# Attention and a two-layer MLP: the third tile by seven block products, with its loads, scores and totals in another order

## The chip, the core and the metric

The kernel runs on one core of a Trainium2 chip. The metric is the device time of one execution in microseconds (us). The core has five engines that run beside each other, each through its own queue in program order: TensorE (PE, matrix products into the accumulation memory PSUM), VectorE (DVE), ScalarE (ACT), GpSimd (POOL) and SyncE (SP), which in this kernel issues nearly all transfers between the device memory and the core. An instruction that waits holds up everything behind it in its queue.

## The reference

`q`, `k` and `v` have 8 batches, 8 heads, 576 rows and 64 columns. Each head attends within chunks of 64 rows, 9 chunks to a batch. The result, 4608 rows of 512, goes through two weight matrices with an exact GELU between them.

```python
scores = scale * np.matmul(q_c, k_c.transpose(0, 1, 2, 4, 3))   # chunks of 64 rows
scores = scores - np.max(scores, axis=-1, keepdims=True)
attn = np.exp(scores)
attn = attn / (np.sum(attn, axis=-1, keepdims=True) + 1e-09)
out = np.matmul(attn, v_c)
# x: (4608, 512), the heads side by side
h = x @ w_in                                                   # 512 -> 2048
g = 0.5 * h * (1.0 + erf(h * inv_sqrt2))
return (g @ w_out).astype(np.float32)                          # 2048 -> 512
```

## The kernel before

**Tiles.** The 4608 rows are worked in 9 tiles of 512 rows. Tile `t` from 0 to 7 holds the first 8 chunks of batch `t`; tile 8 holds the ninth chunk of all batches. The code runs a loop over `t` from 1 to 8, with tile 0 ahead of it. In each pass the PE does two long products for tile `t`:

- mm1 (`mm1_slot`, L414): 16 groups of 4 matmuls, each group 128 of the 2048 columns of `h`; ACT takes a group's PSUM bank through the Gelu into `h` (L421). The banks come from `ps_mm`, which has three.
- mm2: `h` times `w_out`. Tiles 0 to 2 do it directly (`mm2_slot`, L550): 16 slots of 4 matmuls of 512 columns; four slots make one block of 128 rows, which `rows_out` copies out of PSUM (ACT for the first three blocks, DVE for the fourth, L572) and `store` (L567) writes. Tiles 3 to 8 do it with `mm2_seven` (L476): a Winograd-style scheme with seven block products instead of eight, each of 16 matmuls of 256 columns (L519). It needs sums of blocks of `h`, made by DVE during mm1 (`g_sum`, L455), and sums of blocks of `w_out`, made once during mm1 of tile 1 (`weight_sum`, L444).

**Attention for later tiles.** The attention of tile `n = t + 1` is worked in between the matmuls of tile `t`. Its steps are: load `q` and `k` (`load_qk`, L103), cast to bf16 on POOL (`pool_cast_qk`), transpose by a DMA (`flip`, L191, one each for q and k), scores (`quad_S`, 64 small matmuls, L227), `exp` on ACT (L234), partial sums on DVE (L249, L252), totals and their reciprocals (`quad_total`, DVE L265 and L267 with small ACT copies L262 and L272 between them), spreading (`quad_rc`, L276), V (`load_v_rows`, cast by POOL, L200), attention times V (`quad_av`, L283) and the scaled result into `x` (`quad_x`, DVE L290), which mm1 of tile `n` reads.

**What sets the order.** Each engine's queue is in the order in which the code writes the instructions. Within mm1 and mm2 that order is written by hand: the dictionary `e1` says which steps stand ahead of which group of mm1, `e2` which stand ahead of which step of mm2. `phase` (L596) walks through both. At the head of each pass stand the transfers, all on SP's queue. Only the buffers are given out by the framework: a tile of a pool gets one of the pool's buffers when its former content has been read for the last time. The output buffers `y` (`ypool`) are four.

At the head of pass 1 the code puts on SP's queue: transpose of q of tile 2, half of V of 2, transpose of k of 2, three stores of tile 0 (`held`), the other half of V, then q and k of tile 3, q and k of tile 4, the transposes of tile 3, V of tile 3. The fourth row block of tile 0 is done inside mm1 of tile 1 (`last_av`), and its store stands behind all of these. Pass 2 begins with the transposes of tile 4.

In passes 1 and 2 the attention of tiles 2 and 3 is done wholly within mm2 of the tile before, and the scores of tile 4 stand in the last quarter of mm2 of tile 2 (`e2[12]`), its totals at group 3 of mm1 of tile 3 (`e1[3]`). From pass 3 on the scores of tile `t + 2` stand at the start of mm2 of tile `t`, its totals at step 10 of it, and the AV of tile `t + 1` at its start.

**The end.** The 512 rows of tile 8 go to eight separate places of 64 rows, four to a block. `store_block` writes four pieces for each of the first three blocks on SP; `last_piece` writes the last block, in two parts, half on SP and half on ACT's queue.

Of the kernel before, what the change touches and what calls it, by code (L numbers as in the profile page):

```python
# [11 lines left out]
def kernel(  # L12
# [9 lines left out]
    nc = tc.nc  # L22
    P = 128
    f32 = mybir.dt.float32
# [397 lines left out]

    NQ = 4
    T0 = 2
    joint = {T0: 3 * NQ}

    HF = FF // 2
    HD = d_model // 2
# [47 lines left out]
    def mm2_seven(t, hooks):  # L476

        st = tiles[t]

        def raw(r, c):  # L480
            return lambda f, m: st["h"][:, HF * c + f, HD * r + P * m:HD * r + P * (m + 1)]

        def summed(i):
            n = HF // 2
            return lambda f, m: st["S", i][f // n][:, f % n, P * m:P * (m + 1)]

        bank, kept = {}, {}

        def keep(name, of):
            kept[name] = ypool.tile([P, HM, HD], f32, tag="y", name="kept")  # L490
            nc.scalar.copy(kept[name][:], bank[of][:])  # L491

        def done(r, c, of, plus):
            y_sb = ypool.tile([P, HM, HD], f32, tag="y", name="y_sb")
            nc.vector.tensor_tensor(y_sb[:], bank[of][:], kept[plus][:], op=ADD)  # L495
            store_block(t, r, c, y_sb)

        def last():
            y_sb = ypool.tile([P, HM, HD], f32, tag="y", name="y_sb")
            nc.scalar.copy(y_sb[:], bank["a"][:])  # L500
            store_block(t, 1, 0, y_sb)

        steps = [("a", raw(0, 0), w_block(0, 0), lambda: keep("p1", "a")),
                 ("b", raw(0, 1), w_block(1, 0), lambda: done(0, 0, "b", "p1")),
                 ("a", summed(2), t_sum(2), lambda: keep("u2", "a")),
                 ("d", summed(1), t_sum(1), lambda: keep("p5", "d")),
                 ("a", summed(3), t_sum(3), lambda: done(1, 1, "a", "p5")),
                 ("d", summed(4), w_block(1, 1), lambda: done(0, 1, "d", "u2")),
                 ("a", raw(1, 1), t_sum(4), last)]
        for s, (name, left, right, then) in enumerate(steps):  # L510
            fresh = name not in bank
            for m in range(HM):
                for u in hooks.get(HM * s + m, ()):
                    u()
                if fresh and m == 0:
                    pool, tag = (ps_mm, "mm") if name == "d" or t == NT - 1 else (ps_tp, "tp")
                    bank[name] = pool.tile([P, HM, HD], f32, tag=tag, name="y_ps")
                for f in range(HF):
                    nc.tensor.matmul(bank[name][:, m], left(f, m), right[:, f],  # L519
                                     start=(fresh and m == 0 and f == 0),  # L520
                                     stop=(f == HF - 1), skip_group_check=True)
                if t == NT - 1 and s == len(steps) - 1:
                    last_piece(t, m, bank["a"][:, m])
            if not (t == NT - 1 and s == len(steps) - 1):
# [12 lines left out]

    def last_piece(t, m, y_ps):
        y_sb = ypool.tile([P, HD], f32, tag="y", name="y_sb")
        n = HD // 2  # L540
        if m == 0:
            nc.scalar.copy(y_sb[:], y_ps)
        else:
            nc.vector.tensor_copy(y_sb[:, 0:n], y_ps[:, 0:n])
            nc.scalar.copy(y_sb[:, n:HD], y_ps[:, n:HD])
        for i in range(P // CH):
            m0 = ((HM + m) * (P // CH) + i) * S + MT
            (nc.sync if i == 0 else nc.scalar).dma_start(out[m0:m0 + CH, 0:HD], y_sb[i * CH:(i + 1) * CH])

    def mm2_slot(t, ms, qt):  # L550
        st = tiles[t]
        if qt == 0:
            pool, tag = (ps_tp, "tp") if joint.get(t) == ms * NQ else (ps_mm, "mm")
            st["y_ps", ms] = pool.tile([P, d_model], f32, tag=tag, name="y_ps")
        y_ps = st["y_ps", ms]
        for f in range(qt * FF // NQ, (qt + 1) * FF // NQ):
            nc.tensor.matmul(y_ps[:], st["h"][:, f, ms * P:(ms + 1) * P], w_out_sb[:, f, :],  # L557
                             start=(f == 0), stop=(f == FF - 1))
        if qt == NQ - 1:
            if t > 0 or ms < 3:  # L560
                rows_out(t, ms)
# [93 lines left out]
    with tc.manual_schedule():  # L655
# [184 lines left out]
_INS = ['q', 'k', 'v', 'moe_w_in', 'moe_w_out']  # L840
_OUTS = [((4608, 512), 'float32')]
# [25 lines left out]
```

## Time and profile before

| | |
|---|---|
| median of 3 runs | 285.04 us (282.73 to 286.26) |
| the profiled execution's own time | 286.06 us |
| its span in the profile | 284.0 us |
| PE busy | 270.3 us, 95% |
| ACT, DVE, POOL busy | 180.7, 159.3, 91.7 us |
| read and written | 36.70 MB and 9.44 MB |

All times of the trace are from one execution and count from the start of its span. The granted clock of PE is given as a share of full speed. A line such as `L421` is a line of the kernel. In lists of waits, the engine and line behind an arrow are what ended an idle time.

### The profile page before, as it was taken

How to read it: one execution, taken by the hardware profiler on the slowest of the kernel's cores; microseconds unless marked ns; L12 is line 12 of the kernel's file. 1: busy time of each engine (PE TensorE's matmuls, PEld its weight loads, DVE VectorE, ACT ScalarE, POOL GpSimd, SP SyncE). 2: the span in 40 equal slices, each digit the busy share in tenths (PEclk: the TensorE clock that was granted, in tenths of full speed). 3: DMA queues.
4: the chain of work that ended last, by engine and by line, in shares of the span. 5: the costliest groups of instructions: out<-in, count | busy, mean ns of one | idle time of the engine just before them, and what ended most of it. 6: DMA issues, size and time to landing. Idle time of an engine off the chain costs nothing.

```text
span 284.0 us, 6437 instructions
## 1 busy us (share of the span) xinstructions
PE 270.3 (95%) x2589; PEld 160.7 (57%) x2589; DVE 159.3 (56%) x267; ACT 180.7 (64%) x370; POOL 91.7 (32%) x146
## 2 busy tenths in 40 slices
PE   6799999999999999799999999999999999999991
PEld 2464455444444444248844874587458745864781
DVE  5865358835900299448915992598159816311620
ACT  3766758877647667666676657757775766347410
POOL 6868778831542206304404610451011000000000
PEclk9999999999999999899999999999999999999998
DMA  7999998999789799999999998979430310130024
GB/s 222 253 360 402 393 362 234 226 254 239 179 235 244 238 262 240 241 212 255 220 285 237 168 204 177 176 168 260 107 84 2 113 35 2 39 111 0 2 46 102
DMA packets 122477, 53.89 MB, mean 190 GB/s; under 512 B 97872, under 2 KB 118352, under 8 KB 122448
## 3 DMA queue, kind: packets, MB, share of 16 engines
q1 hardware_dynamic: 122288, 53.36, 72.8%
q8 instruction: 20, 0.33, 0.5%
q10 hardware_dynamic: 160, 0.13, 0.2%
q14 instruction: 9, 0.07, 0.1%
HBM read 36.70 MB, written 9.44 MB: 162 GB/s over the span
## 4 chain that ended last, share of the span: by engine, by line
PE 87%; ACT 3%; DVE 2%; DMA 2%; POOL 2%; SPq 1%; issue 1%; DVEq 0%; ACTq 0%
PE h_ps L419 41%; PE y_ps L519 25%; PE y_ps L557 11%; PE y_ps L593 3%; PE h_ps L409 2%; DMA arrival<-in_k_dram 2%; POOL v_bd L169 2%; PE s_ps L227 1%; PE av_ps L283 1%; SPq L114 1%; PE tp L175 1%; ACT h L421 1%; DVE x L290 1%; PE av_ps L374 1%; ACT y_sb L572 1%
## 5 line engine op out<-in xcount | busy, mean ns | idle before, releaser
L419 PE MATMUL h_ps<-x,w_in_sb 128*128 128x512 bf16 x548 | 121.9, 383 | 2.2 <-ACT h L421 2.2
L421 ACT ACTIVATE h<-h_ps 128x512 bf16<-128x512 f32 x137 | 80.9, 598 | 38.0 <-PE h_ps L419 37.7
L419 PEld LDWEIGHTS <-w_in_sb 128*128 128x128 bf16 x548 | 54.0, 99 | 67.7 <-issue 5.0
L164 POOL CAST q_nat<-arrival 128x512 bf16<-128x512 f32 x31 | 19.9, 682 | 62.9 <-DMA arrival<-in_q_dram 41.9
L557 PE MATMUL y_ps<-w_out_sb,h 128*128 128x512 bf16 x144 | 32.4, 379 | 0.0
L519 PEld LDWEIGHTS <-h 128*128 128x128 bf16 x288 | 27.9, 98 | 5.1 <-issue 1.2
L200 POOL CAST v_nat<-arrival 128x1024 bf16<-128x1024 f32 x14 | 15.0, 1075 | 48.4 <-DMA arrival<-in_v_dram 30.2
L461 DVE TENSOR_TENSOR s_sb<-h 128x2048 bf16<-128x2048 bf16 x6 | 7.4, 1226 | 35.8 <-ACT h L421 35.8
L491 ACT COPY kept<-y_ps 128x512 f32<-128x512 f32 x18 | 10.6, 586 | 23.2 <-PE y_ps L519 22.0
L653 ACT ACT_TABLE_LOAD x18 | 23.1, 1283 | 1.1 <-PEq L851 0.7
L519 PE MATMUL y_ps<-w_out_sb,h 128*128 128x256 bf16 x192 | 22.0, 272 | 0.7 <-DVE x L290 0.5
L557 PEld LDWEIGHTS <-h 128*128 128x128 bf16 x144 | 13.5, 98 | 15.5 <-issue 0.2
L519 PE MATMUL y_ps<-v_bd,k_bd 128*128 128x256 bf16 x192 | 21.9, 273 | 0.0
L162 POOL CAST k_nat<-arrival 128x512 bf16<-128x512 f32 x28 | 21.1, 785 | 0.9 <-DMA arrival<-in_k_dram 0.9
L290 DVE TENSOR_TENSOR x<-av_ps,rc 128x512 bf16<-128x512 f32 x28 | 18.5, 682 | 4.8 <-PE av_ps L283 4.5
L519 PEld LDWEIGHTS <-k_bd 128*128 128x128 bf16 x192 | 18.8, 98 | 2.2
L252 DVE TENSOR_REDUCE part<-pt 128x16 f32<-128x512 bf16 x28 | 19.2, 686 | 1.0
L495 DVE TENSOR_TENSOR y_sb<-y_ps,kept 128x512 f32<-128x512 f32 x18 | 12.2, 678 | 12.9 <-PE y_ps L519 7.3
L474 DVE TENSOR_TENSOR k_bd<-h 128x1024 bf16<-128x1024 bf16 x12 | 9.2, 770 | 15.1 <-ACT h L421 15.1
L262 ACT COPY part<-part 32x32 f32<-32x32 f32 x56 | 12.3, 219 | 6.8 <-DVE part L252 6.0
L249 DVE STREAM_TRANSPOSE pt<-pT 128x256 f32<-128x256 f32 x28 | 12.2, 435 | 7.5 <-ACT pT L234 7.5
L234 ACT ACTIVATE pT<-s_ps 128x512 bf16<-128x512 f32 x28 | 14.8, 600 | 0.0
(97 smaller groups left out, 302.8 us busy)
## 6 DMA issues: line engine op xcount, KB each, us to landing
out_dram<-y_sb SPq DMA_DIRECT2D x32, 256.0 KB, 2.8
arrival<-in_v_dram SPq DMA_DIRECT2D x58, 128.0 KB, 3.3
arrival<-in_k_dram SPq DMA_DIRECT2D x28, 256.0 KB, 6.4
arrival<-in_q_dram SPq DMA_DIRECT2D x7, 1024.0 KB, 7.6
arrival<-in_moe_w_out_dram SPq DMA_DIRECT2D x4, 1024.0 KB, 11.7
arrival<-in_moe_w_in_dram SPq DMA_DIRECT2D x6, 512.0 KB, 7.8
arrival<-in_v_dram SPq DMA_DIRECT2D x28, 64.0 KB, 2.7
arrival<-in_q_dram SPq DMA_DIRECT2D x4, 256.0 KB, 5.0
```

The costliest lines, as they stand in the source:

```text
L162: copy(st[nm][:, :, g], st[nm + "f"][:, :, g].rearrange("p (q r) d -> p q r d", r=2))
L164: copy(st[nm][:, g].rearrange("p j r d -> p r j d"), st[nm + "f"][:, 2 * g:2 * g + 2])
L200: copy(st["v"][:, r::2], st["vf"][:, r::2])
L234: nc.scalar.activation(pT[:].rearrange("p u (c j) -> p u c j", j=J), s_ps[g2][c][:].rearrange("p u (j c) -> p u c j", j=J), Act.Exp, scale ...
L252: nc.vector.tensor_reduce(st["part", g2][:, c, :, :, 0], pt[:].rearrange("p n e u -> p n u e"), axis=mybir.AxisListType.X, op=mybir.AluOpT ...
L262: nc.scalar.copy(part[g2][QD * s:QD * (s + 1), :, :, :, 1], part[g2][QD * o:QD * (o + 1), :, :, :, 0])
L290: nc.vector.tensor_tensor(x.rearrange("p n (e u) -> p n e u", u=2), st["av"][g2][c][:].rearrange("p n (e u) -> p n e u", u=2), st["rc", 2 ...
L419: nc.tensor.matmul(h_ps[:], w_in_sb[:, ks, f * P:(f + 1) * P], tiles[t]["x"][:, ks, :], start=(ks == 0), stop=(ks == KS - 1))
L421: nc.scalar.activation(tiles[t]["h"][:, f, :], h_ps[:], Act.Gelu)
L519: nc.tensor.matmul(bank[name][:, m], left(f, m), right[:, f], start=(fresh and m == 0 and f == 0), stop=(f == HF - 1), skip_group_check=True)
L557: nc.tensor.matmul(y_ps[:], st["h"][:, f, ms * P:(ms + 1) * P], w_out_sb[:, f, :], start=(f == 0), stop=(f == FF - 1))
L653: nc.scalar.activation(act_scratch[:], rest[:, 0:1], func)
```

## The change

It alters the order of work around tiles 1 to 3, and how the last tile is stored.

- **Tile 2 by seven products.** `phase` is called with `seven=t >= T0`, so that mm2 of tile 2 goes through `mm2_seven` too. The special bank of `joint` goes.
- **Head of pass 1.** SP's order is now: q and k of tile 3, the transposes of tile 2, all of V of tile 2, the three stores of tile 0, the transposes of tile 3, q and k of tile 4, V of tile 3. POOL casts q and k of tile 3 ahead of V of tile 2.
- **Scores.** The scores of tile 3 stand at step 13 of mm2 of tile 1 (they stood at step 0 of mm2 of tile 2), and the table load for the Gelu moves behind them, to step 15. Pass 2 has the steps of the later passes: AV of tile 3 and scores of tile 4 at the start of mm2, the totals of tile 4 at step 10.
- **Totals.** The totals of tile 3 stand at group 6 of mm1 of tile 2, its spreading at group 8. In all passes from there on the first sum of `h` stands at group 10 of mm1 in place of 9.
- **Banks.** In `mm2_seven` the banks of tile 7 come from `ps_mm`. In tile 8 the bank `a` becomes a pair of banks from `ps_at`, and copies and sums of it go by halves.
- **The last stores.** Blocks of tile 8 go out in two transfers instead of four, one on SP, one on ACT's queue. The last block is copied in halves of 128 columns by DVE and ACT, stored by SP and ACT.

```diff
+        apart = t == NT - 1
+
+        def fresh_bank(name):
+            if apart and name == "a":
+                pair = [ps_at.tile([P, HD], f32, tag="at", name="y_ps") for _ in range(HM)]
+                bank[name] = [(slice(m, m + 1), pair[m][:].unsqueeze(1)) for m in range(HM)]
+                return
+            pool, tag = (ps_tp, "tp") if name != "d" and t + 2 < NT else (ps_mm, "mm")
+            bank[name] = [(slice(0, HM), pool.tile([P, HM, HD], f32, tag=tag, name="y_ps")[:])]
...
         def done(r, c, of, plus):
             y_sb = ypool.tile([P, HM, HD], f32, tag="y", name="y_sb")
-            nc.vector.tensor_tensor(y_sb[:], bank[of][:], kept[plus][:], op=ADD)
+            for m, y_ps in bank[of]:
+                nc.vector.tensor_tensor(y_sb[:, m], y_ps, kept[plus][:, m], op=ADD)
             store_block(t, r, c, y_sb)
...
-        for m in range(HM):
+        for i, eng in enumerate((nc.sync, nc.scalar)):
+            b0 = HM * r * (P // CH) + i
+            eng.dma_start(out_b[b0:b0 + 3:2, MT:S, cols].rearrange("b p d -> p b d"), y_sb[i * CH:(i + 1) * CH])
+
+    out_b = out.rearrange("(b s) d -> b s d", s=S)
+
+    def last_piece(t, m, y_ps):
+        n = HD // HM
+        b0 = (HM + m) * (P // CH)
+        for c, (copy, eng) in enumerate(((DV, nc.sync), (AC, nc.scalar))):
+            y_sb = ypool.tile([P, n], f32, tag="y", name="y_sb")
+            copy(y_sb[:], y_ps[:, n * c:n * (c + 1)])
             for i in range(P // CH):
-                m0 = ((HM * r + m) * (P // CH) + i) * S + MT
-                nc.sync.dma_start(out[m0:m0 + CH, cols], y_sb[i * CH:(i + 1) * CH, m])
...
+                eng.dma_start(out_b[b0 + i, MT:S, n * c:n * (c + 1)], y_sb[i * CH:(i + 1) * CH])
...
             if t == 1:
-                flip(2, "q")
-                load_v_rows(2, (0,))
-                flip(2, "k")
+                for nm in "qk":
+                    load_qk(3, nm)
+                flip_qk(2)
+                load_v_rows(2)
                 for ms, y_sb in held:
                     store(0, ms, y_sb)
                 held.clear()
-                load_v_rows(2, (1,))
+                pool_cast_qk(3)
+                flip_qk(3)
             elif t == T0:
                 flip_qk(t + 2)
             if n < NT:
                 cast_v_rows(n, PO)
-            if t == 1:
-                bring_qk(t + 2)
-                bring_qk(t + 3)
-                flip_qk(t + 2)
-            if t > 1 and t + 3 < NT:
+            if t + 3 < NT:
                 bring_qk(t + 3)
...
-                e2 = {0: [exp, lambda: quad_S(n)], 3: [total], 5: [gelu],
+                e2 = {0: [exp, lambda: quad_S(n)], 3: [total],
                       7: [av, lambda: quad_x(n, 0, 0)]
                          + [u for m in range(1, G)
-                            for u in (lambda m=m: quad_rc(n, m // 2, m % 2), lambda m=m: quad_x(n, m // 2, m % 2))]}
-            elif t == T0:
-                e2 = {0: [exp, lambda: quad_S(n)], 3: [total],
-                      8: [lambda m=m: quad_rc(n, m // 2, m % 2) for m in range(1, G)],
-                      12: [av] + xs + [lambda: quad_S(n + 1, True)], 13: [flip_next], 15: [gelu]}
+                            for u in (lambda m=m: quad_rc(n, m // 2, m % 2), lambda m=m: quad_x(n, m // 2, m % 2))],
+                      13: [lambda: quad_S(n + 1)], 15: [gelu]}
             else:
...
-                e1 = {9: [lambda: g_sum(t, 3)], 13: g[0]}
+                e1 = {10: [lambda: g_sum(t, 3)], 13: g[0]}
...
-                    if t == T0 + 1:
-                        e1[3] = [total]
-                    e1[5] = [lambda m=m: quad_rc(n, m // 2, m % 2) for m in range(1, G)]
+                    if t == T0:
+                        e1[6] = [total]
+                    e1[8 if t == T0 else 5] = [lambda m=m: quad_rc(n, m // 2, m % 2) for m in range(1, G)]
...
-            phase(t, e2, first=5 if t == 1 else 0, extra1=e1, seven=t > T0)
+            phase(t, e2, first=5 if t == 1 else 0, extra1=e1, seven=t >= T0)
```

More of the change, by code (lines that the diff above doesn't have):

```diff
@@ L424 @@
     T0 = 2
-    joint = {T0: 3 * NQ}
     HF = FF // 2
@@ L487, in mm2_seven, with region @@
         bank, kept = {}, {}
+        apart = t == NT - 1
[6 more added lines that the diff above has]
+            bank[name] = [(slice(0, HM), pool.tile([P, HM, HD], f32, tag=tag, name="y_ps")[:])]
+        def region(name, m):
+            return bank[name][m][1][:, 0] if len(bank[name]) > 1 else bank[name][0][1][:, m]
         def keep(name, of):
             kept[name] = ypool.tile([P, HM, HD], f32, tag="y", name="kept")
-            nc.scalar.copy(kept[name][:], bank[of][:])
+            for m, y_ps in bank[of]:
+                nc.scalar.copy(kept[name][:, m], y_ps)
         def done(r, c, of, plus):
             y_sb = ypool.tile([P, HM, HD], f32, tag="y", name="y_sb")
-            nc.vector.tensor_tensor(y_sb[:], bank[of][:], kept[plus][:], op=ADD)
+            for m, y_ps in bank[of]:
+                nc.vector.tensor_tensor(y_sb[:, m], y_ps, kept[plus][:, m], op=ADD)
             store_block(t, r, c, y_sb)
@@ L499, in last @@
             y_sb = ypool.tile([P, HM, HD], f32, tag="y", name="y_sb")
-            nc.scalar.copy(y_sb[:], bank["a"][:])
+            nc.scalar.copy(y_sb[:], bank["a"][0][1])
             store_block(t, 1, 0, y_sb)
@@ L515, in mm2_seven @@
                 if fresh and m == 0:
-                    pool, tag = (ps_mm, "mm") if name == "d" or t == NT - 1 else (ps_tp, "tp")
-                    bank[name] = pool.tile([P, HM, HD], f32, tag=tag, name="y_ps")
+                    fresh_bank(name)
                 for f in range(HF):
-                    nc.tensor.matmul(bank[name][:, m], left(f, m), right[:, f],
-                                     start=(fresh and m == 0 and f == 0),
+                    nc.tensor.matmul(region(name, m), left(f, m), right[:, f],
+                                     start=(fresh and f == 0 and (m == 0 or len(bank[name]) > 1)),
                                      stop=(f == HF - 1), skip_group_check=True)
-                if t == NT - 1 and s == len(steps) - 1:
-                    last_piece(t, m, bank["a"][:, m])
-            if not (t == NT - 1 and s == len(steps) - 1):
+                if apart and s == len(steps) - 1:
+                    last_piece(t, m, region("a", m))
+            if not (apart and s == len(steps) - 1):
                 then()
@@ L532, in store_block @@
             return
-        for m in range(HM):
-            for i in range(P // CH):
-                m0 = ((HM * r + m) * (P // CH) + i) * S + MT
-                nc.sync.dma_start(out[m0:m0 + CH, cols], y_sb[i * CH:(i + 1) * CH, m])
[L538 to L548, printed above, removed]
+        for i, eng in enumerate((nc.sync, nc.scalar)):
[8 more added lines that the diff above has]
+            copy(y_sb[:], y_ps[:, n * c:n * (c + 1)])
+            for i in range(P // CH):
+                eng.dma_start(out_b[b0 + i, MT:S, n * c:n * (c + 1)], y_sb[i * CH:(i + 1) * CH])
     def mm2_slot(t, ms, qt):
@@ L552, in mm2_slot @@
         if qt == 0:
-            pool, tag = (ps_tp, "tp") if joint.get(t) == ms * NQ else (ps_mm, "mm")
-            st["y_ps", ms] = pool.tile([P, d_model], f32, tag=tag, name="y_ps")
+            st["y_ps", ms] = ps_mm.tile([P, d_model], f32, tag="mm", name="y_ps")
         y_ps = st["y_ps", ms]
```

## The prediction

> **What bounds the kernel now.** I read the page first, then busy time by stage, then the chain of waits around the tile that changes, then the queue that issues the transfers. Tiles are numbered 0 to 8 as `t` in the code; "mm1(3)" is the first product of tile 3, "mm2(3)" its second. The change touches mm2(1), all of tile 2, mm1(3), and the end.
>
> ```profile
> span 284.0 us, 6437 instructions
> ...
> DMA  7999998999789799999999998979430310130024
> ```
>
> Each digit of the DMA row is a fortieth of the span, 7.1 us. None of the first 28 is below 7, and most are 9: up to about 170 us there is little slack on transfers. TensorE (PE) sets the end, so the next view is PE by stage (window, its length, PE busy, PE weight loads, DVE, ACT, POOL, granted clock, DMA share, GB/s).
>
> ```profile
> 110.28:127.97 17.69, 15.66 (x73) 6.56 (x74) 9.65 (x18) 11.30 (x27) 5.16 (x8) 0.90 1.04 221
> 127.97:141.55 13.58, 13.58 (x242) 12.20 (x242) 12.62 (x24) 8.81 (x23) 6.21 (x10) 1.00 1.02 234
> ...
> 238.38:251.95 13.57, 13.03 (x177) 11.68 (x178) 6.36 (x10) 5.33 (x8) 0.00 (x0) 1.00 0.13 43
> ```
>
> The first row is mm1(3): it takes 17.69 us, with PE busy in 15.66 of them at a clock of 0.90. The second is mm2(3), the first tile done by seven products, with the scores and AV of later tiles in it: 13.58 us without a gap. The third is mm2(7), 0.54 us of it idle. The chain of waits (start, us, what) shows where the time of mm1(3) goes and what the pieces cost:
>
> ```profile
> 64.36 0.64 PE s_ps L227 x64
> ...
> 71.82 7.88 PE y_ps L557 x36
> 79.70 13.81 PE h_ps L419 x64
> ...
> 114.47 0.23 DVE total L265
> ...
> 116.84 0.61 ACT h L421
> ...
> 117.49 10.48 PE h_ps L419 x40
> ...
> 129.20 12.35 PE y_ps L519 x112
> ```
>
> A full-speed mm1 is 13.81 us (mm1(2)), 0.863 for each of its 16 groups. In mm1(3) PE waits: the totals of the next tile's softmax sit on DVE and ACT in front of a Gelu, and from DVE's first total (114.47) to PE's restart (117.49) pass 3.02 us. The 40 matmuls after it take 10.48 instead of 40/64 of 13.81, which is 8.63: 1.85 us more. Two window rows tell why:
>
> ```profile
> 115.46:117.49 2.03, 0.00 (x1) 0.00 (x0) 2.00 (x6) 1.39 (x6) 1.04 (x1) 1.00 0.96 249
> 117.49:121.30 3.81, 3.81 (x11) 1.37 (x11) 0.58 (x1) 2.12 (x4) 1.04 (x1) 0.56 1.27 202
> ```
>
> PE stood still for 2.03 us, and was then granted 0.56 of its clock for 3.81 us. Nearly all of mm1(3)'s excess of 3.88 us is this wait and this slow stretch (2.03 + 1.85). It is what the change can take away.
>
> **What the change saves if nothing new waits.** In tile 2, 64 matmuls of 512 columns (7.88/36 = 0.219 each, 14.0 us) become 112 of 256 (12.35): 1.65 us. The stall in mm1(3) goes, since the totals of tile 4 move into mm2(2), as the later tiles have it. Stage by stage: mm1(2) now starts at 79.70 and would start 0.64 later, as the scores of tile 3 move ahead of it, at 80.34; then 13.81, a mm2(2) like the row of mm2(3), 13.58, and mm1(3) at full speed, 13.81, end at 121.5. Now it ends at 127.97. So 6.4 us are to be had.
>
> **What is queued in front of it.** The price is in the order of SP's queue, which issues nearly all transfers, and of DVE's. SP (start, us, what):
>
> ```profile
> 45.11 7.13 SPq L124 DMA_DIRECT2D arrival<-in_k_dram  x4
> 53.32 1.74 SPq L194 DMA_TRANSPOSE q_t<-q_nat  x1
> 55.17 2.22 SPq L124 DMA_DIRECT2D arrival<-in_v_dram  x4
> 58.53 1.32 SPq L194 DMA_TRANSPOSE k_t<-k_nat  x1
> ...
> 83.12 3.08 SPq L194 DMA_TRANSPOSE q_t<-q_nat  x1
> 86.29 1.76 SPq L194 DMA_TRANSPOSE k_t<-k_nat  x1
> ...
> 93.48 5.04 SPq L567 DMA_DIRECT2D out_dram<-y_sb  x5
> 98.62 1.71 SPq L194 DMA_TRANSPOSE q_t<-q_nat  x1
> 100.43 1.84 SPq L194 DMA_TRANSPOSE k_t<-k_nat  x1
> ```
>
> The five stores at 93.48 are the last rows of tile 0 and the four row blocks of tile 1, in that order; the one of tile 0 is issued from the middle of mm1(1) in the code, so in SP's queue it stands behind all loads of the head of loop pass 1. DVE shows what that costs:
>
> ```profile
> 97.47 0.69 DVE L572 COPY y_sb<-y_ps 128x512 f32<-128x512 f32 x1 [19.51 <-DMA out_dram<-y_sb]
> ```
>
> This is the copy of tile 1's last row block out of PSUM. There are four output buffers; the other three hold tile 1's first blocks, whose stores come later still, so it waits for tile 0's last store to land, 3.99 us after its issue. DVE stands for 19.51 us. Today that is free: mm1(2) runs its full 13.81 beside it and asks nothing of DVE. After the change it does: the totals of tile 3 are put ahead of group 6 of mm1(2), then three reciprocal spreads, then the sums of `h` for the seven products, all behind this copy. ACT takes part in the totals, so its Gelus of groups 6 to 15 wait behind its copies, and PE waits for their banks. The change moves nothing of that store: q, k of tile 3, transposes of tile 2, V of 2, three stores, transposes of 3, q, k of 4, V of 3 are the same transfers as now, in another order, and all still ahead of it.
>
> When does it land? Now SP issues it 41.24 us after it was done with k of tile 2 (52.24). Two pauses in that stretch go, because SP has q and k of tile 3 to issue while POOL still casts tile 2: 52.24 to 53.32 and 57.39 to 58.53, together 2.22. That gives 91.3. The bounds: how busy the transfer engines are in that stretch,
>
> ```profile
> 52.24:93.48 41.24, 41.24 (x317) 18.90 (x318) 17.54 (x26) 27.75 (x56) 18.26 (x25) 1.00 0.93 229
> ```
>
> 0.93, so that without a gap the same transfers need 38.4 us, to 90.6; and the four transposes of tiles 2 and 3, whose issue varies (ns, least, median, most):
>
> ```profile
> L194 SPq DMA_TRANSPOSE q_t<-q_nat x4: 1714/2408/4164, 53.3 to 117.5; - x4
> L194 SPq DMA_TRANSPOSE k_t<-k_nat x4: 1324/1802/1872, 58.5 to 121.8; - x4
> ...
> DMA to landing us min/median/max: 3.7/3.9/6.2
> ```
>
> They take 7.9 us now (1.74 + 1.32 + 3.08 + 1.76), 12.1 if both pairs are at the longest, 4.2 more: 95.5. I take 91.0, near the lower end, because in both orders the same transfers run, and 3.99 to landing: 95.0.
>
> The sum from there. DVE's copy 0.69, totals to PE's restart 3.02: 98.7. Before that PE has done groups 0 to 7 (the Gelus of 6 and 7 are stuck in two of three PSUM banks, the third holds the row block) and group 8 when the copy frees that bank; seven remain, 6.04: 104.8. PE has then stood for some 8 us but for one group, so the slow stretch of mm1(3) is to be expected here too, 1.85: 106.6. mm2(2) 13.58 and mm1(3) 13.81 bring 134.0 against 127.97: **6.0 us later**. From there on nothing but the two ends below differs.
>
> What this wait covers, so that I cost it at nothing: the transposes of tile 2 go out behind q and k of tile 3, about 0.5 + 7.2 after 52.24, so k's lands at 52.24 + 7.1 (a k load) + 2.4 + 3.9 = 65.6 or a little later, and its scores start 1.3 us or more after 64.36; the scores of tile 3 (0.64) and waits of V of tile 2 behind POOL's new casts come on top. PE reaches the end of group 7 near 80.34 + 1.3 + 6.9 = 88.5, some 10 us ahead of 98.7. If the wait on DVE were gone, these and one more would count: the transposes of tile 4, today at 98.62, are wanted for scores at the start of mm2(2) instead of its last quarter. The sum of `h` that moves from group 9 to 10 is 0.86 us later and wanted at the fifth of seven products: nothing.
>
> **The ends.** In mm2(7) the first bank now comes from another pool than the one AV uses; the 0.54 us idle go. At the very end:
>
> ```profile
> 277.58 1.03 PE L519 MATMUL y_ps<-v_bd,h 128*128 128x256 bf16 x8 [0.46 <-ACT y_sb L542]
> 280.42 1.18 SPq L548 DMA_DIRECT2D out_dram<-y_sb  x2
> ```
>
> The last 8 matmuls wait 0.46 for a copy from their bank; with a bank of their own they don't. SP gets to the last two stores only at 280.42, behind the earlier blocks' stores, 0.59 each, so the last is issued at 281.01. Afterwards ACT's queue is the longer: from 277.12 a copy (at most that 0.46), two stores 1.18, a copy 0.46, one store 0.59, so its last is issued at 279.8: 1.2 us earlier, the 0.46 in it. From both sides: nothing, if ACT's stores of the block before push these back as far as SP's do today, and 2.0 if ACT is free. Sum of both ends: 1.7 us saved.
>
> Net 6.0 - 1.7 = 4.3 us. The profiled execution took 286.06 (span 284.0), which becomes 290.4. It lies 1.0 above the median of the runs, 285.04, which becomes **289.3**.
>
> **Rivals.**
> *The clock holds (0.10).* The row above charges 1.85 us after a gap of 2.03 us. The Trainium skill, "TensorE: Matmul & The Clock Gate", section "HAM oscillation", says that gaps over about 3.4 us are what re-throttles, and Part 1 that the window of that length runs freely; this trace shows a throttle after 2.03 us, so the row decides. If group 8 splits the stand here into two gaps that don't trip it, the sum is 2.4 us over now: 287.5.
>
> *The store lands early, and only the transposes of tile 4 bind (0.08).* SP would have to run far faster than in any row; then DVE is free by group 8, and SP reaches the transposes at 91.0 plus four stores of about 1.0, issues k's 2.4 later and has it landed 3.9 after that, at 101.3. Scores to the end of mm2(2) are about 13.0, mm1(3) 13.81: 128.1, as now, and only the ends are saved: 283.5.
>
> *Nothing waits (0.07).* Both must be early: 6.4 + 1.7 less, 276.9. For it: the work on PE is indeed less. Against: the order of SP's queue.
>
> *Slower (0.20).* One mechanism, the transposes behind a full load queue: 4.16 + 1.87 for each of two pairs instead of 7.9 for both. Every microsecond goes straight through store, copy, totals and PE. At 4.2 more the end is 293.5; it decides from 1.4 us on, a landing after 96.4.
>
> That the change doesn't do what it says can be left out: the diff sets the order outright.
>
> **How the numbers follow.** My forecast has 0.55, and with landings from 93.4 to 96.4 its own range is 287.7 to 290.7. A measurement of this kernel can't tell 2% from no change, 5.7 us here: 279.3 to 290.7 is "the same". Slower: the fourth rival and a tenth of the forecast, 0.25. Faster: the third rival and a little of the second, 0.08. The rest, 0.67, is the same. The range 283 to 293.5 leaves out the third rival and what goes beyond the fourth's price.
>
> **What would show it.** Right: in mm1(2) a wait of DVE for an out store of well over 10 us ahead of the total, ACT idle before a part or across copy, PE idle some 8 us after group 7 and a clock near 0.5 behind it; mm1(3) at 13.8; no idle at the start of mm2(7). Wrong: an out store that lands before 90 us; PE busy through mm1(2); a wait for k_t ahead of the scores in mm2(2) in its place; a clock of 1.00 after the stand; ACT's queue ending after 281.

## The result, and the profile after

The changed kernel takes 292.99 us (median of 4 runs, 291.62 to 293.88); the kernel before beside it 285.15. The ratio is 1.028, with a 95% interval from 1.021 to 1.036: slower. The forecast was 289.3 with a range of 283.0 to 293.5; it gave 0.67 to "the same" and 0.25 to slower. A few executions of most kernels are over 1.5% above the fastest of the same kernel; a median here is of all runs, a ratio of the others alone, so that it isn't exactly the quotient of two medians. The profiled execution took 293.88, its span is 292.1 where it was 284.0. Two rows of the page after (in fortieths of the span, 7.3 us each):

```profile
PEclk9999999997999579999999999999999999999998
DMA  6999999997999998889939894989641220130014
```

Before, the granted clock dipped once before the last slice, in slice 16 (113.6 to 120.7 us). Now it dips twice: slice 9 (65.7 to 73.0 us, the head of mm2(1)) and slices 13 and 14 (94.9 to 109.5 us, mm1(2)). The transfer engines are nearly as full as they were, up to about 146 us.

The list of waits after the change (who waited for whom: us in total, times, longest) has the wait that the prediction named, and who stood behind it:

```profile
DVE y_sb L581 <- DMA out_dram<-y_sb: 9.2, 1, 9.2
...
PE h_ps L419 <- DVE y_sb L581: 5.2, 1, 5.2
...
PE s_ps L227 <- DMA k_t<-k_nat: 3.4, 2, 3.1
```

DVE waits 9.2 us for an out store. PE waits 5.2 us for the copy that DVE makes when the store has landed. The chain of waits after (start, us, what) has them in their order:

```profile
93.05 3.77 DMA out_dram<-y_sb
96.92 0.69 DVE y_sb L581
97.61 0.14 DVE total L265
...
99.88 0.61 ACT h L421
100.53 1.01 PE h_ps L419 x2
...
109.53 0.64 PE av_ps L283 x64
```

Store of tile 0 issued at 93.05, landed 96.9, copy, totals, Gelu, PE at 100.53: link by link the chain of the prediction, 1.8 us later than it said. Then mm2(2) runs as forecast, and mm1(3) too. The stages after (window, its length, PE busy, and so on as before; the granted clock is the third number from the end):

```profile
92.49:97.66 5.17, 0.00 (x0) 0.00 (x0) 0.74 (x2) 0.73 (x4) 2.08 (x2) 0.84 0.82 264
97.66:101.06 3.40, 2.39 (x6) 0.81 (x6) 3.30 (x9) 1.98 (x7) 0.00 (x0) 0.50 0.87 220
101.06:104.50 3.44, 3.22 (x9) 1.18 (x9) 1.17 (x2) 1.36 (x3) 0.00 (x0) 0.50 1.07 215
104.50:106.50 2.00, 2.00 (x7) 0.69 (x5) 0.02 (x1) 0.83 (x2) 0.00 (x0) 0.57 1.02 328
109.53:123.10 13.57, 13.57 (x242) 12.19 (x242) 12.89 (x23) 8.30 (x22) 6.48 (x9) 1.00 0.94 223
123.10:137.08 13.98, 13.87 (x71) 6.14 (x74) 5.84 (x8) 10.66 (x19) 5.55 (x8) 1.00 0.90 230
```

PE stands from 92.49, does group 8 at half clock, stands again, and runs at half clock to about 106.2. The stall of mm1(3) is gone (17.69 us before, 13.98 now); it ends at 137.08 all the same, where it ended at 127.97. From there to the end nothing else than the ends differs: the profile gives 292.1 - 284.0 = 8.1 us, of them 9.1 lost by 137.08, 0.6 won at mm2(7), 0.3 at the end of the kernel and 0.1 between.

### The profile page after: what moved, and what is told of

Its sections match the earlier page's. It is cut to its first block, busy times and chain, and to the rows that moved or that the text cites. A ratio compares the mean times of both kernels' runs of the same rounds, so it can differ in the third digit from the quotient of the medians.

```text
span 292.1 us, 6525 instructions
## 1 busy us (share of the span) xinstructions
PE 270.8 (93%) x2614; PEld 166.3 (57%) x2637; DVE 168.6 (58%) x278; ACT 181.3 (62%) x373; POOL 93.4 (32%) x146
## 4 chain that ended last, share of the span: by engine, by line
PE 61%; DMA 16%; SPq 11%; POOL 4%; DVE 2%; issue 2%; ACT 1%; POOLq 0%; DVEq 0%; ACTq 0%
PE h_ps L419 30%; PE y_ps L531 28%; SPq L124 8%; DMA arrival<-in_moe_w_out_dram 8%; DMA arrival<-in_k_dram 3%; DMA out_dram<-y_sb 2%; DMA arrival<-in_q_dram 2%; SPq L194 2%; POOL v_bd L169 2%; PE av_ps L283 1%; SPq L114 1%; PE s_ps L227 1%; POOL w_out_sb L651 1%; DMA arrival<-in_v_dram 1%; DVE rc L276 1%
## 5 line engine op out<-in xcount | busy, mean ns | idle before, releaser
L531 PEld LDWEIGHTS <-h 128*128 128x128 bf16 x336 | 32.4, 98 | 4.3
L503 ACT COPY kept<-y_ps 128x512 f32<-128x512 f32 (+1 forms) x23 | 12.5, 549 | 25.5 <-PE y_ps L531 23.0
L531 PE MATMUL y_ps<-w_out_sb,h 128*128 128x256 bf16 x224 | 25.6, 272 | 0.0
L531 PE MATMUL y_ps<-v_bd,k_bd 128*128 128x256 bf16 x224 | 25.6, 273 | 0.0
L531 PEld LDWEIGHTS <-k_bd 128*128 128x128 bf16 x224 | 21.9, 98 | 2.5
L162 POOL CAST k_nat<-arrival 128x512 bf16<-128x512 f32 x28 | 22.6, 846 | 0.1
L473 DVE TENSOR_TENSOR k_bd<-h 128x1024 bf16<-128x1024 bf16 x14 | 11.6, 829 | 18.9 <-ACT h L421 18.9
L508 DVE TENSOR_TENSOR y_sb<-y_ps,kept 128x512 f32<-128x512 f32 (+1 forms) x22 | 14.3, 649 | 11.9 <-PE y_ps L531 7.2
L566 PE MATMUL y_ps<-w_out_sb,h 128*128 128x512 bf16 x76 | 19.4, 406 | 0.4 <-issue 0.3
L272 ACT COPY across<-rb 64x16 f32<-64x16 f32 x28 | 5.7, 202 | 14.6 <-DVE rb L267 14.4
```

The costliest lines, as they stand in the source:

```text
L162: copy(st[nm][:, :, g], st[nm + "f"][:, :, g].rearrange("p (q r) d -> p q r d", r=2))
L531: nc.tensor.matmul(region(name, m), left(f, m), right[:, f], start=(fresh and f == 0 and (m == 0 or len(bank[name]) > 1)), stop=(f == HF - ...
```

## The experiments

Each ran beside the kernel before on the same chip. What a run is compared with is the ratio to that, since the medians of the kernel before lay between 283.5 and 285.2.

| run | us | before beside it | ratio | 95% interval |
|---|---|---|---|---|
| the change | 292.99 | 285.15 | 1.028 | 1.021 to 1.036 |
| change, copy's own buffer | 286.97 | 284.15 | 1.008 | 1.004 to 1.012 |
| change, store early | 286.65 | 284.15 | 1.008 | 1.004 to 1.012 |
| before, copy's own buffer | 283.06 | 284.15 | 0.999 | 0.997 to 1.002 |
| before, new end | 283.32 | 284.15 | 0.998 | 0.995 to 1.002 |
| own buffer, transposes between | 287.16 | 283.45 | 1.013 | 1.009 to 1.018 |
| own buffer, totals in pieces | 286.99 | 283.45 | 1.012 | 1.007 to 1.017 |
| own buffer, all repairs | 284.89 | 283.45 | 1.003 | 0.999 to 1.007 |
| before, pieces and new end | 280.76 | 283.45 | 0.991 | 0.988 to 0.995 |
| own buffer, pieces, no k of tile 3 | 282.59 | 283.62 | 0.996 | 0.993 to 1.000 |
| change, no k of tile 3 | 287.98 | 283.62 | 1.015 | 1.010 to 1.020 |
| before, no k of tile 3 | 283.95 | 283.62 | 1.001 | 0.997 to 1.004 |
| before, pieces | 281.95 | 283.62 | 0.995 | 0.992 to 0.997 |

### Is it the wait for the store?

The first takes away what the copy waits for: a buffer of its own.

```diff
+        if t == 1 and ms == 3:
+            y_sb = work.tile([P, d_model], f32, tag="t1", name="y_sb", bufs=2)
+        else:
+            y_sb = ypool.tile([P, d_model], f32, tag="y", name="y_sb")
-        y_sb = ypool.tile([P, d_model], f32, tag="y", name="y_sb")
```

> The changed kernel, but the copy of tile 1's last row block goes to a buffer of its own (one that the softmax of tile 1 has done with), so it need not wait for tile 0's store. My theory, that this wait holds DVE, and through the totals ACT and PE: DVE's wait of 9.22 us ahead of the copy goes, mm1(2) takes about 15.1 us (13.8 and some 1.3 for the totals ahead of group 6) in place of 24.1, and then the transpose of k of tile 4 is what mm2(2) waits for, 1 to 3 us; mm1(3) ends near 129 in place of 137.1; 283.5 to 287 us. Rival, that the totals ahead of group 6 hold ACT by themselves and the copy only stands beside them: mm1(2) stays over 20 us and the time over 290.

The second leaves the buffers alone and moves the store forward in SP's queue.

```diff
+            def loads():                # q, k of tile t + 3 and V of tile t + 2, as before
+                ...
+            if t > 1:
+                loads()
...
             if t == 1:
                 mm1_slices(1, (mm, at, at, mm, mm),
...
+                loads()
```

> The changed kernel with its four output buffers, but q, k of tile 4 and V of tile 3 are put on SP's queue behind mm1(1)'s beginning, so that the last store of tile 0 stands ahead of them. Theory, that the place in SP's queue decides when that store lands: it is issued near 80 in place of 93.05 and has landed when the copy comes, near 85; the rest as with a buffer of its own, 283.5 to 287 us. Rival, that the load on the transfer engines decides and not the place in the queue: it lands after 90 all the same, DVE waits over 5 us, over 288.

DVE's copy with a buffer of its own, and PE in mm1(2) (timelines: start, us, what, and the idle time ahead of it where there was any):

```profile
86.40 0.68 DVE L584 COPY y_sb<-y_ps 128x512 f32<-128x512 f32 x1
```
```profile
94.50 7.89 PE L419 MATMUL h_ps<-x,w_in_sb 128*128 128x512 bf16 x28 [2.03 <-ACT h L421]
```

and PE with the store early, which SP issued at 79.76:

```profile
95.28 6.20 PE L419 MATMUL h_ps<-x,w_in_sb 128*128 128x512 bf16 x28 [2.02 <-ACT h L421]
...
102.94 0.71 PE L227 MATMUL s_ps<-q_t,k_t 64*64 64x64 bf16 x64 [0.81 <-DMA k_t<-k_nat]
```

In both the copy follows the work before it without a wait, and both ratios are the same to a tenth of a per cent: 2.0 of the 2.8% go. Buffer and place in the queue are two handles of one wait, and that it is this wait is shown. What is left in mm1(2) is a stand of 2.0 us, the totals' own, as mm1(3) had it before the change: the change moved that stall, it didn't remove it. With the stand, mm1(2) takes 18.1 us in the first of the two traces and 16.4 in the second, not the 15.1 expected: the stand is 2.0 us in place of 1.3, and behind it the clock was low in the first trace only (last section).

The same buffer in the kernel before asks whether the wait was free there.

> The kernel before, with the copy of tile 1's last row block in a buffer of its own. My prediction costs the wait of 19.51 us of DVE at nothing there: the wait goes and the time stays within 0.7 us of 285. Rival, that DVE's late start costs already before the change (partial sums and totals of tile 3 come later in mm2(2)): 1 to 2 us less, 283 to 284.

0.999 (0.997 to 1.002): it was. A wait of 19.5 us that costs nothing became one of 9.2 us that costs 2%, because other work was queued behind it.

### Does each microsecond of the store go through?

k of tile 3 isn't loaded but taken from tile 2's, which lies in the chip.

```diff
-                for nm in "qk":
-                    load_qk(3, nm)
+                load_qk(3, "q")
+                tiles[3]["kf"] = tiles[2]["kf"]
+                tiles[3]["k"] = ld.tile([P, G, J, 2, D], bf16, tag="k", name="k_nat")
```

> The changed kernel as it is, without the load of k of tile 3 (taken from tile 2's as above). Theory, that SP's queue alone sets when the store of tile 0 lands, and that each microsecond of it goes straight through to the end: the store lands near 90 for 96.9, DVE still waits for it, mm1(2) ends 6 to 7 us earlier, 285.5 to 287.5 us. Rival, that something else than this store sets PE's restart in mm1(2): under 3 us gained, over 290.

> The kernel before, without the load of k of tile 3 in the same way, as the control of the two others. Theory: its order leaves the transfers time enough, so nothing is gained, within 1 us of the kernel before. Rival: 1 MB less is worth several us in any order: 280 or less.

DVE and PE of the change without that load:

```profile
92.14 0.69 DVE L581 COPY y_sb<-y_ps 128x512 f32<-128x512 f32 x1 [7.99 <-DMA out_dram<-y_sb]
```
```profile
104.40 0.71 PE L283 MATMUL av_ps<-pT,v_nat 64*64 64x64 bf16 x64
```

The store landed at 92.1 in place of 96.9, 4.8 us earlier; mm1(2) ended at 104.4 in place of 109.5, 5.1 earlier. The median is 5.0 less, the profile's span 5.7 (292.1 to 286.4); by the ratios, 1.028 and 1.015, it is 3.9 us, give or take 2.6 by their intervals. So in the trace it goes straight through, and the times agree with that without showing it to the microsecond. The kernel before gains nothing from the same cut (1.001): its order has the time. I had expected 6 to 7 us. SP's queue shows why only 4.8 came:

```profile
54.79 5.79 SPq L194 DMA_TRANSPOSE q_t<-q_nat  x1
```

The load that is gone took 7.4 us of SP, but the transpose that now stands right behind the load of q takes 5.8 us to issue where it took 3.1. In all the store is issued 3.8 us earlier (89.25 for 93.05), and it lands 2.9 us after that where it took 3.9.

### What holds the repaired change back?

Two waits are left after the first repair: PE's 2.5 us for k_t of tile 2 at the head of mm2(1), and the totals' 2.0 us. One run each:

```diff
-                for nm in "qk":
-                    load_qk(3, nm)
-                flip_qk(2)
+                load_qk(3, "q")
+                flip(2, "q")
+                load_qk(3, "k", ns=(0, 1))      # half of the rows
+                flip(2, "k")
+                load_qk(3, "k", ns=(2, 3))
```

> The changed kernel with the copy's own buffer, and the transposes of tile 2 put between the loads of tile 3 (q load, transpose of q, half of k, transpose of k, other half) in place of behind both. Theory: the wait of PE for k_t of tile 2 at the head of mm2(1) (2.5 us with the own buffer alone) goes, with the slow clock behind it, and mm1(2) starts about 4 us earlier (near 80.5 for 84.2); but the k_t of tile 4 lands near 101.5 as before, so that most of it comes back as a wait at the head of mm2(2), 2 to 3 us; net 1 to 2 us under the own buffer alone. Rival, that what is won at mm2(1) stays won, because the transfers are early enough: 4 us under it.

The second cuts the totals into pieces: `total_a` has a half's copies into `part`, total and reciprocal, `total_b` the copies that wait for that reciprocal.

```diff
-                        e1[6] = [total]
+                        e1.update({4: [lambda: total_a(n, 0)], 6: [lambda: total_a(n, 1)],
+                                   7: [lambda: total_b(n, 0)], 8: [lambda: total_b(n, 1)]})
-                    e1[8 if t == T0 else 5] = [lambda m=m: quad_rc(n, m // 2, m % 2) for m in range(1, G)]
+                    e1[9 if t == T0 else 5] = [lambda m=m: quad_rc(n, m // 2, m % 2) for m in range(1, G)]
```

> The changed kernel with the copy's own buffer, and the totals of tile 3 in four pieces ahead of groups 4, 6, 7 and 8 of mm1(2), the small copies that wait for DVE's reciprocals two groups and more behind these. Theory: the 2.03 us for which PE stands in mm1(2) is the totals' own price, which the change only moved from mm1(3): it goes, mm1(2) is 13.8 to 14.3 us; then k_t of tile 4 is waited for, up to 1.5 us; net 1 to 2.5 us under the own buffer alone. Rival: ACT is late for another reason, and PE stands as long, only elsewhere in mm1(2): no change.

Neither gained anything: 1.013 and 1.012 against 1.008 with the buffer alone. With the transposes in between (SP's queue, then PE):

```profile
53.25 6.70 SPq L194 DMA_TRANSPOSE q_t<-q_nat  x1
```
```profile
66.11 0.71 PE L227 MATMUL s_ps<-q_t,k_t 64*64 64x64 bf16 x64 [0.52 <-DMA k_t<-k_nat]
...
75.45 0.73 PE L283 MATMUL av_ps<-pT,v_nat 64*64 64x64 bf16 x63 [2.07 <-POOL v_nat L200]
```

the wait for k_t shrinks to 0.5 us, and 2.1 us for V of tile 2 take its place 9 us later. With the totals in pieces, PE's queue reads

```profile
67.38 1.07 PE L227 MATMUL s_ps<-q_t,k_t 64*64 64x64 bf16 x64 [3.99 <-DMA k_t<-k_nat]
...
88.93 11.77 PE L439 MATMUL h_ps<-x,w_in_sb 128*128 128x512 bf16 x51 [0.17 <-DVE y_sb L604]
...
102.48 0.71 PE L227 MATMUL s_ps<-q_t,k_t 64*64 64x64 bf16 x64 [1.14 <-DMA k_t<-k_nat]
```

so mm1(2) runs through (the totals' stand is theirs, and gone), but PE then waits for k_t of tile 4. The 3.99 us ahead of it are no work of the edit: up to there the order is that of the run with the buffer alone, where the same wait is 2.54 us. So waits for transfers differ by 1.5 us from execution to execution, and one trace can't show a gain of that size here. The scores of tile 4 start at 102.9, 102.9, 105.0 and 102.5 us in the four runs so far, whatever is repaired ahead of them.

All of it together, with the transposes of tile 4 ahead of the stores and buffers of their own for the last pieces:

```diff
-            elif t == T0:
-                flip_qk(t + 2)
...
             if t + 2 < NT:
                 load_v_rows(t + 2)
+            if t == 1:
+                flip_qk(4)
...
-            y_sb = ypool.tile([P, n], f32, tag="y", name="y_sb")
+            y_sb = work.tile([P, n], f32, tag="rc", name="y_sb", bufs=4)
```

> The changed kernel with the copy's own buffer, transposes of tile 2 between the loads, totals in pieces, the transposes of tile 4 ahead of the stores of tiles 0 and 1 in SP's queue, and buffers of their own for the four last pieces. If the waits named so far are all there is: PE through mm2(1), mm1(2) and mm2(2) with under 2 us idle, mm1(3) ends near 125, the span ends 5 us or less behind the last matmul, 279 to 282 us, below the kernel before. Rival, that the transfers bound this stretch whatever the order: mm1(3) ends near 128 and the time is 283 to 285.

1.003 (0.999 to 1.007), level with the kernel before; PE waited 1.97 us for k_t of tile 2 and 2.26 for V of tile 2, and mm1(3) ended at 128.2. The numbers are the rival's: in no order of the change tried here does this stretch end earlier. That the transfers bound it is only argued by this. The last run on it takes transfers away instead of reordering them (k of tile 3 as above, on the run with pieces):

> The changed kernel with the copy's own buffer and the totals in pieces, and k of tile 3 is not loaded: it is cast from the k of tile 2 that lies there (so the scores of tile 3 are of the wrong k; 1 MB and some 7 us of SP's queue less, all else the same). Theory, that after the two waits on DVE and ACT only the transfers of this stretch hold the change back: no wait for k_t ahead of mm2(1) nor mm2(2), mm1(3) ends near 122 (the 121.5 of the prediction's sum without waits) in place of 129.3, 278.5 to 281 us. Rival, that the order of the work on the engines costs as much as the transfers: mm1(3) ends after 126, over 283.

```profile
98.73 0.71 PE L227 MATMUL s_ps<-q_t,k_t 64*64 64x64 bf16 x64 [2.06 <-DMA k_t<-k_nat]
...
125.52 0.71 PE L303 MATMUL av_ps<-pT,v_nat 64*64 64x64 bf16 x64
```

0.996, 1.6% under the same kernel with the load, and mm1(3) ends at 125.5, between what the two theories said. Ahead of this wait for k_t of tile 4 the same view has 0.64 and 0.55 us for those of tiles 2 and 3, and 0.18 for a copy: 3.4 us in all, without which mm1(3) would end at 122.1, near the 121.5 of the prediction's sum without waits. So the 6.4 us are there on PE, and the waits that keep them are for transfers; this one cut brings them 3.2 us forward (SP issues the store of tile 0 at 89.22, with the load at 92.38), not all that is needed. The 122.1 is worked out from waits, not run.

### The end, and a version that beats both

The end alone, with the change's `mm2_seven` (but tile 7's bank as before), `store_block` and `last_piece` put into the kernel before:

> The kernel before, with only the end of the change: pair of banks and half copies in tile 8, blocks stored in two transfers on SP and ACT, the last block in halves on both. The prediction's price: 1.2 us less from the start of the last mm2 to the end of the span (18.24 to 17.0). Rival, from the trace after the change: the last copy on ACT waits for an output buffer, so that the end of the span follows the last matmul by 5.8 us in place of 5.4, and only 0.3 us are saved in the stage.

0.998 (0.995 to 1.002): the time doesn't tell 1.2 us from nothing. The trace does: from the first matmul of the last mm2 to the end of the span it has 18.1 us, the kernel before 18.4, so 0.3 are saved, as the rival had it. After the change, PE's last matmuls have lost their wait, but ACT's queue (timeline, ACT, the change) reads

```profile
283.40 2.65 ACTq L547 DMA_DIRECT2D out_dram<-y_sb  x2
286.14 0.27 ACT L556 COPY y_sb<-y_ps 128x128 f32<-128x128 f32 x1 [4.32 <-DVE y_sb L556]
286.44 1.36 ACTq L558 DMA_DIRECT2D out_dram<-y_sb  x2
288.33 0.27 ACT L556 COPY y_sb<-y_ps 128x128 f32<-128x128 f32 x1 [1.92 <-DMA out_dram<-y_sb]
288.62 1.13 ACTq L558 DMA_DIRECT2D out_dram<-y_sb  x2
```

The last copy waits 1.92 us for one of the four output buffers: again a copy behind a store. The first of the two copies is late as well: DVE copies its half of the same rows at 285.56, but ACT issues two stores of the block before until 286.05. The last matmul ends at 286.4, the span 5.7 us later; before it was 5.4.

The totals' stall can be had without the change. The kernel before with pieces ahead of groups 4 to 7 of mm1(3), alone, and with the new end (own buffers for the last pieces) and the bank of tile 7:

```diff
-                    if t == T0 + 1:
-                        e1[3] = [total]
-                    e1[5] = [lambda m=m: quad_rc(n, m // 2, m % 2) for m in range(1, G)]
+                    if t == T0 + 1:
+                        e1.update({4: [lambda: total_a(n, 0)], 5: [lambda: total_a(n, 1)],
+                                   6: [lambda: total_b(n, 0)], 7: [lambda: total_b(n, 1)]})
+                    e1[8 if t == T0 + 1 else 5] = [lambda m=m: quad_rc(n, m // 2, m % 2) for m in range(1, G)]
```

> The kernel before with only the totals of tile 4 in four pieces, ahead of groups 4 to 7 of mm1(3). Theory: the 2.03 us in which PE stands there go but for some tenths, and the slow clock with them where it follows: 1.5 to 3 us under the kernel before. Rival: the gain of the run with pieces and the new end came from the end: under 0.7 us.

> The kernel before, with the totals of tile 4 in pieces ahead of groups 4 to 7 of mm1(3), the change's end with buffers of its own for the last pieces, and the bank of tile 7 from the pool of mm1. Theory: the 2.03 us of mm1(3) go (and a slow clock where it follows), 0.5 in mm2(7), and the end follows the last matmul by less than 5.4 us: 2.5 to 4 us under the kernel before, 280 to 281.7. Rival, that the stall comes back elsewhere in mm1(3) and the end is bound by the landing of the last store whatever its buffer: within 1 us of before.

0.995 (0.992 to 0.997) and 0.991 (0.988 to 0.995): by the ratios 1.4 and 2.5 us, the first just under what was expected, the second its least. In both the stand is 0.34 us in place of 2.03. For the second, on PE:

```profile
116.11 7.33 PE L439 MATMUL h_ps<-x,w_in_sb 128*128 128x512 bf16 x31 [0.34 <-ACT h L441]
```

At 280.8 us it is the fastest kernel of the study, 0.9% under the kernel before and some 3.6% under the change. With buffers of their own the last copy no longer waits for a store, yet the span's end follows the last matmul by 5.4 us as in the kernel before: now two stores stand ahead of that copy in ACT's queue. From the first matmul of the last mm2 to the end it is 17.8 us, where the change has 18.1: the buffers are worth 0.3. Which part of the 0.4% between the two runs is the end and which the bank of tile 7 wasn't separated.

## Why the prediction was right, and where its sizes were off

**The stall in front, right.** DVE's copy waits for tile 0's store; totals, Gelu and PE stand behind it; two handles that remove this wait give back 2.0%, and moving the landing by 4.8 us moves the end of mm1(2) by 5.1. The cover claimed for the kernel before holds (0.999). The sizes were off, nearly all in one direction. The likeliest outcome, "the same", didn't come, and the range held by 0.5 us. Its upper end was priced for a late landing alone; half of what filled it is the landing, the other half terms that the range took for sure. That they stopped short of 293.5 is luck.

**The landing, 1.9 us off.** The step that failed is "I take 91.0, near the lower end, because in both orders the same transfers run". The store was issued at 93.05. SP's queue after the change:

```profile
60.26 3.09 SPq L194 DMA_TRANSPOSE q_t<-q_nat  x1
63.45 2.06 SPq L194 DMA_TRANSPOSE k_t<-k_nat  x1
...
74.01 2.93 SPq L194 DMA_TRANSPOSE q_t<-q_nat  x1
77.04 3.04 SPq L194 DMA_TRANSPOSE k_t<-k_nat  x1
```

The two pairs take 11.1 us, where the prediction had 7.9 in hand and 12.1 as the upper bound. The two pauses of 2.22 us went as forecast, but the stretch from the end of tile 2's loads to this store took 41.35 us (from 51.70), where it took 41.24 before: 229 GB/s in both, at a DMA share of 1.01 for 0.93. So the lower bound of 90.6, which took a share of 0.93 for room to fill, was no bound: rows of the prediction itself show up to 1.27. The longer transposes are the mechanism of the rival "slower", three quarters of it: the landing at 96.9 is beyond the 96.4 from which it was said to decide. From there to PE's restart it took 3.6 us, summed 3.7.

**The slow clock, 1.1 us off.** From 100.53 the seven groups took 9.0 us, 2.96 over their 6.04; the term was 1.85, the size seen after one short stand. The clock fell to 0.50 within the first stand, at 96.0, and came back at 106.2: 10.2 us, three times the 3.4 us of the single short stand (last section). The rival "the clock holds" didn't happen: group 8 between the two stands didn't keep the clock up.

**mm2(2) and mm1(3), right.** 13.57 and 13.98 for 13.58 and 13.81.

**What the wait covers, 3.8 us off, at no cost.** The prediction had mm1(2) begin at 81.6 (80.34 + 1.3); it began at 85.42. At the head of mm2(1) PE reads

```profile
67.36 0.71 PE L227 MATMUL s_ps<-q_t,k_t 64*64 64x64 bf16 x64 [3.10 <-DMA k_t<-k_nat]
```

so k_t of tile 2 is waited for 3.1 us in place of 1.3 (the landing at 65.6 left out the 0.5 us that the load of q takes of SP), and the clock is low behind it. So two of the signs came smaller than written down: DVE's wait is 9.2 us and not "well over 10", PE stands 5.2 and 1.0 us around group 8 and not "some 8". The store landed later still, so the total didn't feel it; the repaired kernel did.

**The ends, 0.8 us off.** The step that failed is "so its last is issued at 279.8: 1.2 us earlier"; the stage from the start of the last mm2 shrank by 0.3 only (18.24 to 17.93). It let ACT be free when the last block's first half is ready, and ACT was still issuing two stores of the block before, for 0.6 us more: the bound that the same paragraph names and sets aside (read from the queue, with no run of its own). And it left out that the new pieces take four more tiles from four output buffers, the first half of the same argument, forgotten at its end; that is the smaller part, since buffers of their own win back 0.3. The 0.54 of mm2(7) came (26.79 for mm2(7) and mm1(8) in place of 27.38).

Together 1.9 + 1.1 + 0.2 + 0.8 - 0.1, less the 0.1 won in between, is the 3.8 us between the 4.3 forecast and the 8.1 measured.

**The second rival had the next wait, and its place.** "Only the transposes of tile 4 bind" gave 283.5; with the first wait removed the kernel stood at 287, since the totals' stand, which I had counted as saved, came along, and the wait for tile 2's transposes, which the first wait had covered, came out.

## What to carry to other kernels

A wait that costs nothing is a fact about what is queued behind it: before work is put on an engine, look whether that engine already stands there, and for what; here a store at the end of a queue of prefetches held a buffer, the buffer held a copy, and the copy held an engine that had been idle. A stall that is moved to another place isn't removed; cutting the step that stalls into pieces that fit under the next engine's lead removed it, in the old order. Where transfers fill the time, an order that wants the same bytes earlier only moves the wait, and a run that takes the bytes away tells this from a bad order.

## What the runs showed of the hardware that I had not expected

**A stand of 2 us costs the clock or not by where it falls.** Stands of PE from 1.97 to 2.07 us occur ten times in the 14 traces, the first ending at 66 us. After four of them PE got 0.52 to 0.62 of its clock over the next 3.4 us, after six all of it. The buffer run and the run with the store early show the two cases behind the same wait (windows from PE's restart):

```profile
94.50:97.90 3.40, 3.40 (x9) 1.25 (x9) 1.70 (x2) 1.65 (x4) 0.21 (x1) 0.56 1.07 316
```
```profile
95.28:98.68 3.40, 3.40 (x16) 1.56 (x16) 2.44 (x2) 2.71 (x5) 1.04 (x1) 1.00 1.00 274
```

9 matmuls in one, 16 in the other. The granted clock read in windows of 1 us and less shows what tells them apart. Between 60 and 130 us there are eleven low stretches in the 14 traces, at 0.50 from their beginning to their end. Eight last 3.4 us, two 6.8, and the one after the change 10.2. Within a trace their edges lie whole multiples of 3.41 us apart (falls at 67.56 and 94.88 in the buffer run, 8 times 3.415). So here the clock is set anew every 3.41 us, and these steps don't begin with the stand. (Where a trace has no low stretch there, the steps below are counted back from the fall of the clock behind the last matmul.)

Laid on those steps, in all traces, the clock fell at the end of each step in which PE had stood for 2.03 us or more, and of none in which it had stood for 1.70 or less. In the buffer run all 2.03 us of the stand lie in one step (91.47 to 94.88); with the store early 1.65 lie ahead of an edge at 94.91 and 0.37 behind it. It came back at the end of the first step with 0.33 us or less of standing, and not with 1.2 or more: that is how two stands with group 8 between them made three low steps after the change. In the run of the change without k of tile 3, group 8 still ran at 1.00 behind a stand of 3.94 us; the clock fell 1.2 us after PE's restart.

The kernel before has one such stand, so the 1.85 us that the prediction read from its trace need not be in each of its executions: three other traces with its order of mm1(3) have the stand and no low clock behind it. They end mm1(3) at 125.0, 125.0 and 126.2 us, not at 127.97, so that of the 6.4 us "to be had" about 3.5 to 4.7 are left against them. A stand of 2.03 us that falls anywhere lies within one step with a chance of 1 - 2.03/3.41, about 0.4 (an estimate from these lengths).

The Trainium skill, "TensorE: Matmul & The Clock Gate", Part 1, has the clock decided over a window of 3.4 us that runs freely, and lowered after a whole idle one. The length and the free run agree with these traces; a whole idle window wasn't needed in them, 2.03 us of one was enough, and there the measurement decides.

**What a transpose costs SP depends on what is ahead of it.** Transposes of q of the same size took from 1.5 us to issue to 6.9, the longest right behind the load of a whole q, which itself is issued in 0.8 us. A sum of issue times can't be carried from one order of a queue to another.
